# A Fourier mixing layer and a gated feed-forward network in one kernel: the first two chunks of batch 0 take the weights half by half

## The chip, the cores and the metric

The kernel runs on one core of a Trainium2 chip. The core has five engines with queues of their own: TensorE (PE; PEld are its weight loads), VectorE (DVE), ScalarE (ACT), GpSimd (POOL) and SyncE (SP, which here only issues DMAs). They meet through semaphores. The metric is the device time of one execution in microseconds; the median of three runs of the kernel before is 1980.55 (1979.31 to 1981.25).

## The reference

```python
X = np.fft.fft(x, axis=1)            # x: (8, 3008, 256)
X = np.fft.fft(X, axis=2)
a = X.real.reshape(24064, 256)
gate = 1.0 / (1.0 + np.exp(-(a @ w_gate)))       # w_gate, w_val: (256, 1536)
out = gate * (a @ w_val) @ w_out                 # w_out: (1536, 256)
```

The real part of a two-dimensional Fourier transform of each batch goes through a gated network. The weights arrive as 64-bit floats, everything else as 32-bit.

## The kernel before

**Sequence transform.** For each batch the kernel folds x by the symmetries of cosine and sine and multiplies it with a cosine and a sine table `ST` (lines 392 to 440). The results are rows P ("pk"), Q ("qk") and one extra row e for the feature in the middle ("ek", for batch 0 a whole resident tile; for the others a row in memory, `ed`, that is broadcast chunk by chunk into `ek`). For batch 0 this is done at the start, from tables loaded by `load_table` (line 188): the cosine sums first, then the sine sums, and `evacuate` brings each out of PSUM between weight conversions (lines 682 to 693).

**The feature transform is merged into the weights.** `jobs` (line 204) cuts the three weight matrices into 18 pieces of 256 columns or rows: `(0, c)` of w_gate, `(1, c)` of w_val, `(2, c)` of w_out. A piece is loaded by SP (`weight_load`) and converted from 64 to 32 bits in `weight_round`: two ACT operations (lines 261, 262), three DVE operations (271, 272, 274) and one POOL addition (276). A gate or value piece is then merged with the feature table on TensorE (`merge`, line 290: eight matmul records, two ACT copies into `G1` and `G2`, two small DMAs into `ge`). An output piece is used by `forms`: 11 sums (line 317) and 4 copies (line 315, ACT) of 128x128 blocks for each group of three hidden tiles. For groups 0 and 1 the sums run on POOL, for 2 and 3 on DVE, in parts of six and five.

**The main loop.** The sequence is cut into six chunks of 252 rows (the last 246) a batch, and the 1536 hidden columns into 12 tiles of 128. One step `i` is one hidden tile of one chunk, 576 steps in all. Within a step the order is written out by hand:
- `front_a(i)`: two matmuls of P with `G1` into a PSUM bank "pf";
- `part(i)`: for the first 12 steps DVE adds e (line 523, two operations); later ACT copies with scale 2 (line 520), and the bank was filled with e times `ge` by `seed` one step earlier (line 506, ACT);
- `gate_a(i-1)`, `gate_b(i-1)`: sigmoid (539, ACT), difference (541, or 544 from step 12, DVE), product (556, DVE), second sigmoid (557, ACT), product (558, DVE), and after the second and third tile of a group 7 and 6 sums of blocks on POOL (line 562);
- what is due of the weights (`pre`, `use`, `parts_`);
- `back((i-5)//3, (i-5)%3)`: five of the 15 products of a group of three hidden tiles with the forms `wf` of w_out, into the PSUM tiles "po0" to "po4";
- `front_b(i)`: two matmuls of Q with `G2` onto the same bank.

A chunk is four groups, 12 steps. With its last group the five "po" tiles are copied to `C` by ACT (tiles 0, 2, 4) or DVE (1, 3), line 586, and `finish` puts 20 sums (line 609) and four transposes (line 619) of it into `later`; every step takes two or three of these in turn, on DVE. PSUM has eight banks: five are "po", three are shared by "pf" and the merges' "ps". Three resident tiles hold several things in turn: `x4` (x of the next batch, and weight pieces 10 and on), `os` (output, and e of batch 0) and `c` (C, and weight pieces 7 and 8).

**When the weights are due.** Pieces 0 to 8 are converted before step 0. Pieces 9 to 17 are converted at steps 0 to 8, and a gate or value piece among them is merged at steps 4 to 8, two to four steps after its conversion:

```python
for j in range(9, len(jobs)):
    pre.setdefault(j - 9, []).append(lambda j=j: weight_round(j))
    if KEEP <= j < len(jobs) - 3:
        at(j - 9, lambda j=j: weight_load(j + 3))
for j in range(3, len(jobs)):
    w, c = jobs[j]
    i = (0, 1, 4, 7, 9, 10)[c] if w == 2 else 2 * c - 3 + w
```

**Side work.** `at(i, f)` puts work at the end of step i: the copy of the next batch's x in another order through DRAM (`mirror_x`), its load (`load_x(1)` at step 14), seven small loads `e_load`, the same for the tables, the sums of e on TensorE at step 40 (`e_sums`), and folds of x on POOL (`fold_ops`).

Of the kernel before, what the change touches and what calls it, by code (L numbers as in the profile page):

```python
# [7 lines left out]
F32 = mybir.dt.float32  # L8
I32 = mybir.dt.int32
U32 = mybir.dt.uint32  # L10
AF = mybir.ActivationFunctionType
# [66 lines left out]
def kernel(  # L78
# [49 lines left out]
    def mm(o, l, r, start, stop):  # L128
        nc.tensor.matmul(o, l, r, start=start, stop=stop, skip_group_check=True)  # L129
# [57 lines left out]

    def load_table(t, nq):
        for q in range(0, NQ, nq):
            nc.sync.dma_start(out=ST[0][0:NP, t, q : q + nq], in_=stab[:, t, q : q + nq])  # L190

    def mirror_tables():
        return mirrored(tr, stab, NE)
# [1 line left out]
    def table_again():  # L195

        ST[0] = const.tile([P, 2, NQ, NE + NO], F32, name="st", tag="st")
        for t in range(2):
# [2 lines left out]

    jobs = [(w, c - (w == 2)) for c in range(NPR + 1) for w in range(3)
            if (c if w == 2 else c < NPR)]
    RAW, WS = {}, {}
    shared = {}
    KEEP = 10
# [94 lines left out]
    def forms(g):  # L303

        w = [WO[f // 2].rearrange("p f (a h j) -> p f h a j", h=2, j=TB)[:, f % 2]
             for f in range(3 * g, 3 * g + 3)]
        f = wf[:, g].rearrange("p m (a j) -> p m a j", j=TB)
        engine = nc.gpsimd if g < 2 else nc.vector

        def block(i):  # L310
            return w[i // 2][:, i % 2] if i < 6 else f[:, i - 6]

        def some(lo, hi):
            for i, (a, sign) in enumerate(W_COPIES if lo == 0 else ()):
                nc.scalar.mul(f[:, len(W_SUMS) + i], block(a), float(sign))
            for i, (a, b, op) in list(enumerate(W_SUMS))[lo:hi]:
                engine.tensor_tensor(f[:, i], block(a), block(b), op=(ALU.subtract, ALU.add)[op])  # L317
        return [lambda lo=lo: some(lo, lo + 6) for lo in range(0, len(W_SUMS), 6)]


    W = {}
# [157 lines left out]

    chunks = [(k0, min(CH, -(-(NK - k0) // 3) * 3)) for k0 in range(0, NK, CH)]  # L480
    assert NK <= chunks[-1][0] + chunks[-1][1] <= NK + 1 and NFT == 12
    groups = [(b, c, g) for b in range(B) for c in range(len(chunks)) for g in range(NG)]
    H, SF, EK = {}, {}, {}

    def cut(i):
        b, c, _ = groups[i // 3]
        k0, n = chunks[c]
        f = i % NFT
        return PQE[b], slice(k0, k0 + n), n, f, slice(f * P, (f + 1) * P)

    def e_rows(i):

        b, c, _ = groups[i // 3]
        k0, n = chunks[c]
        EK[i // NFT] = ekp.tile([P, CH], F32, name="ek", tag="ek")[:, 0:n]
        nc.sync.dma_start(out=EK[i // NFT], in_=ed[b : b + 1, k0 : k0 + n].to_broadcast([P, n]))

    PF, AP, Z = {}, {}, {}

    def seed(i):  # L500


        _, _, n, f, _ = cut(i)
        PF[i] = bank("pf").rearrange("p (g n) -> p g n", g=2)[:, :, 0:n]
        for g in range(2 if i >= NFT else 0):
            nc.scalar.activation(PF[i][:, g], EK[i // NFT], AF.Copy, scale=ge[:, g, f : f + 1])  # L506

    def front_a(i):
        (pk, *_), ks, _, _, fs = cut(i)
# [59 lines left out]
    def back(p, part):  # L569

        b, c, g = groups[p]
        n = chunks[c][1]
        R = 2 * n // 3
        last = p == len(groups) - 1
        if part == 0 and g == 0:
            PO[:] = [pso.tile([P, 2 * WC], F32, name=f"po{t}", tag=f"po{t}") for t in range(NB)]
        for at_, (hb, wb) in list(enumerate(PRODUCTS))[part * 5 : part * 5 + 5]:
            t, j = divmod(PLACE[at_], 3)
            mm(PO[t][:, j * R : (j + 1) * R], wf[:, g, wb], block(p, hb), g == 0 and at_ % 3 == 0,
               g == NG - 1)  # L580
            if g == NG - 1 and at_ % 3 == 2:
                if t == 0:
                    C[0] = cp.tile([P, 10 * WC], F32, name="c", tag="c")
                    nc.gpsimd.memset(C[0][:, 15 * R : 15 * R + 40], 0.0)
                if not (last and t == NB - 1):
                    (nc.vector.tensor_copy if t == 1 or t == 3 and not last else nc.scalar.copy)(  # L586
                        C[0][:, 3 * t * R : 3 * (t + 1) * R], PO[t][:, 0 : 3 * R])
        if part == 2:
            del H[p], SF[p]
            if g == NG - 1:  # L590
                finish(b, c, last)

    def finish(b, c, last):
# [1 line left out]
        R = 2 * n // 3  # L595
        more = k0 + n > NK
        nb = -(-n // TB)
        t = C.pop(0)
        queues = (nc.sync, nc.scalar) if last else (nc.sync,)
        os_ = []  # L600

# [56 lines left out]
    for j in range(2):  # L658
        weight_load(j)
    load_x(0)  # L660
    load_table(0, NQ // 2)
    for j in range(2, 6):
        weight_load(j)
    load_table(1, NQ)
    for j in range(6, KEEP):
        weight_load(j)

    def weight_round(*js):
        for j in js:
            weight_parts(j)  # L670
            weight_join(j)
# [12 lines left out]
        for sums, _, _ in cos:  # L684
            sums(*range(i * NQ // 2, (i + 1) * NQ // 2))
    sin = [seq_group(0, blk, 1, other.get((blk, 1))) for blk in range(2)]
    for sums, _, _ in sin:
        sums(*range(NQ))
    evacuate = [then for _, then, _ in cos + sin]
    for then, js in zip(evacuate, ((2, 3, 4), (5,), (), (), (6, 7), (8,))):  # L690
        weight_round(*js)
        then()()
    nc.scalar.dma_start(out=ed[0:1], in_=PQE[0][2][0:1])
    nc.vector.tensor_copy(PQE[0][1][0:1, 0:CH], PQE[0][2][0:1, 0:CH])
    for j in range(KEEP, KEEP + 3):
        weight_load(j)
    weight_use(2)
# [5 lines left out]
        side.setdefault(i, []).extend(fs)  # L703

    pre, use = {}, {}
    for j in range(9, len(jobs)):
        pre.setdefault(j - 9, []).append(lambda j=j: weight_round(j))
        if KEEP <= j < len(jobs) - 3:  # L710
            at(j - 9, lambda j=j: weight_load(j + 3))
    for j in range(3, len(jobs)):
        w, c = jobs[j]
        i = (0, 1, 4, 7, 9, 10)[c] if w == 2 else 2 * c - 3 + w
        use.setdefault(i, []).append(lambda j=j: weight_use(j))


# [2 lines left out]
    calm = lambda lo: (i for i in range(lo, count) if 3 <= i % i0 <= 7)  # L720
    for i, f in enumerate(mirror_x(1)):
        at(i0 - 3 + i // 2, f)
    at(i0 + 2, lambda: load_x(1))
    for b in range(1, B):
        at(i0 + 2 + b, lambda b=b: e_load(b))
    for i, f in enumerate(mirror_tables()):
# [1 line left out]
    at(3 * i0, e_fold)  # L728
    at(3 * i0 + 4, lambda: e_sums()())
    at(3 * i0 + 6, table_again)  # L730
    for i in range(i0, count, i0):
        at(i - 8, lambda i=i: e_rows(i))

    for b in range(B - 1):
        s0 = b * per
        g0 = s0 + 3 * i0 + 4 if b else 5 * i0 + 4


        slots = [i for i in range(s0 - 2 * i0 if b > 1 else s0 if b else 2 * i0, g0) if i % i0 < 4]

        def folds(slots, b=b):
            ops = fold_ops(b + 1, 2)
            for i, f in enumerate(ops):
                at(slots[i * len(slots) // len(ops)], f)
        at(slots[0] - 1, lambda slots=slots, folds=folds: folds(slots))
        at(g0 - 2, lambda b=b: seq_start(b + 1))
        for blk in (1, 0):
            at(g0, *[lambda b=b, blk=blk, what=what: whole(b + 1, blk, what)() for what in range(2)])
        if b < B - 2:
            at(g0 + 1, lambda b=b: load_x(b + 2))  # L750
            for i, f in zip(calm(s0 if b else 3 * i0), mirror_x(b + 2)):
                at(i, f)

    for i in range(count):
# [14 lines left out]
        if i >= 5:  # L769
            back((i - 5) // 3, (i - 5) % 3)  # L770
        front_b(i)
        n = 3 if i >= count - 8 else 2 + i % 2
        for f in later[0:n]:
            f()
        del later[0:n]
# [57 lines left out]
```

## Time and profile before

| | |
|---|---|
| median of three runs | 1980.55 us |
| the profiled execution | 1978.69 us |
| its span | 1976.8 us |
| granted TensorE clock, mean | 0.995 |
| TensorE busy | 1932.9 us (98%) |
| DVE busy | 1518.7 us (77%) |
| ACT busy | 1337.7 us (68%) |
| POOL busy | 1631.4 us (83%) |
| TensorE busy, 60 to 90 us | 8.92, 8.16 and 3.46 us of each 10 |
| TensorE busy, 300 to 1900 us | all of it |

The page counts an engine as busy while an instruction runs on it. A line of the timeline has its start, its length, the engine, the line of the code, the operation, what it writes and reads, and in brackets how long the engine sat idle before it and what it waited for. A line of the waits has the waiting engine and line, what released it, the total in us, how often, and the longest. A line of the windows has the stretch, its length, and for each engine the busy time and the number of instructions. One product of 32-bit floats stands as two matmul records, so a front's two matmuls are "x4". Neighbouring lengths overlap by what a pipeline hides, so the time of a thing is best read from start to start.

### The profile page before, as it was taken

What the parts mean: (1) busy time and instruction counts of PE and PEld (TensorE: products, weight loads), DVE (VectorE), ACT (ScalarE), POOL (GpSimd) and SP (SyncE); (2) the same over time, 40 slices, a digit from 0 to 9 for tenths busy, and PEclk for the clock granted to TensorE, in tenths of its full rate; (3) what the DMA queues carried; (4) which work ended last, traced back from release to release, by engine and by line L of the source; (5) the groups of instructions that cost most, each with busy time, mean ns of one, the idle gap of its engine ahead of it and who ended that gap; (6) DMA issues with size and microseconds to landing.
All of it is one profiled execution on the core that took longest, in us unless ns stands there. A gap on an engine that the chain in (4) does not pass through costs nothing.

```text
span 1976.8 us, 34387 instructions
## 1 busy us (share of the span) xinstructions
PE 1932.9 (98%) x11232; PEld 1788.1 (90%) x11232; DVE 1518.7 (77%) x3177; ACT 1337.7 (68%) x3103; POOL 1631.4 (83%) x2858
## 2 busy tenths in 40 slices
PE   6899999999999999999999999999999999999997
PEld 3689889998999899998999989999899999999997
DVE  7788778886787677786778867787678877777777
ACT  3467657775777667775777757777577766777774
POOL 3879888997889878997889868998688996777776
PEclk9999999999999999999999999999999999999999
DMA  7354413112012020212013021211210110011011
GB/s 267 88 132 93 137 31 110 47 26 77 14 47 58 14 78 14 66 39 77 15 25 80 15 78 23 47 49 22 77 20 14 20 21 14 14 19 22 14 19 27
DMA packets 171444, 101.41 MB, mean 51 GB/s; under 512 B 133890, under 2 KB 163204, under 8 KB 168588
## 3 DMA queue, kind: packets, MB, share of 16 engines
q1 hardware_dynamic: 169294, 98.64, 20.5%
q8 instruction: 90, 1.47, 0.3%
q10 hardware_dynamic: 1940, 0.56, 0.1%
q14 instruction: 88, 0.72, 0.1%
q0 software_dynamic: 32, 0.00, 0.0%
HBM read 74.45 MB, written 50.18 MB: 63 GB/s over the span
## 4 chain that ended last, share of the span: by engine, by line
PE 94%; DMA 2%; DVE 2%; ACT 1%; POOL 1%; issue 0%; ACTq 0%; DVEq 0%; SPq 0%; POOLq 0%
PE pf L129 48%; PE po L129 41%; PE ev L129 4%; DMA st<-in_stab_dram 1%; DMA ge<-G 1%; PE ps L129 1%; PE od L129 1%; DVE wf L317 0%; DMA raw<-in_moe_w_val_dram 0%; DVE ae L523 0%; DVE z L541 0%; POOL sf L562 0%; DVE h L558 0%; POOL wf L317 0%; DVE c L609 0%
## 5 line engine op out<-in xcount | busy, mean ns | idle before, releaser
L562 POOL TENSOR_TENSOR sf<-h 128x168 f32<-128x168 f32 (+1 forms) x960 | 549.3, 591 | 222.0 <-DVE h L558 221.9
L562 POOL TENSOR_TENSOR sf<-h,sf 128x168 f32<-128x168 f32 (+1 forms) x1152 | 657.6, 591 | 58.7 <-DVE h L558 58.7
L129 PE MATMUL pf<-qk,G 128*128 128x252 f32 (+1 forms) x2304 | 582.6, 376 | 3.2 <-DVE ae L523 1.9
L129 PE MATMUL pf<-pk,G 128*128 128x252 f32 (+1 forms) x2304 | 582.9, 376 | 0.0
L558 DVE TENSOR_TENSOR h<-z 128x252 f32<-128x252 f32 (+1 forms) x576 | 301.3, 523 | 350.7 <-ACT z L557 350.1
L506 ACT ACTIVATE pf<-ek,ge 128x252 f32<-128x252 f32 (+1 forms) x1128 | 531.5, 471 | 18.5
L129 PE MATMUL po<-sf,wf 128*128 128x168 f32 (+1 forms) x3072 | 530.1, 306 | 0.0
L520 ACT ACTIVATE ae<-pf 128x504 f32<-128x504 f32 (+1 forms) x564 | 332.6, 590 | 234.4 <-PE pf L129 233.6
L609 DVE TENSOR_TENSOR c<-c 128x168 f32<-128x168 f32 (+1 forms) x949 | 484.8, 542 | 5.5 <-ACT c L586 0.3
L129 PEld LDWEIGHTS pf<-pk,G 128*128 128x128 f32 x2304 | 436.3, 190 | 53.0 <-issue 2.3
L129 PEld LDWEIGHTS po<-sf,wf 128*128 128x128 f32 x3072 | 473.0, 190 | 8.5
L129 PE MATMUL po<-h,wf 128*128 128x168 f32 (+1 forms) x2688 | 475.9, 305 | 2.1 <-ACT a L473 1.6
L129 PEld LDWEIGHTS po<-h,wf 128*128 128x128 f32 x2688 | 427.4, 190 | 19.2 <-ACT a L473 2.0
L129 PEld LDWEIGHTS pf<-qk,G 128*128 128x128 f32 x2304 | 409.9, 190 | 30.0 <-DVE ae L523 2.9
L544 DVE TENSOR_TENSOR z<-ae,pf 128x504 f32<-128x504 f32 (+1 forms) x564 | 374.3, 664 | 17.6 <-ACT h L539 17.1
L539 ACT ACTIVATE h<-pf 128x252 f32<-128x252 f32 (+1 forms) x576 | 218.5, 379 | 164.4 <-PE pf L129 152.7
L557 ACT ACTIVATE z<-z 128x252 f32<-128x252 f32 (+1 forms) x576 | 231.1, 401 | 91.0 <-DVE z L544 59.5
L556 DVE TENSOR_TENSOR h<-h,pf 128x252 f32<-128x252 f32 (+1 forms) x576 | 232.2, 403 | 0.0
L562 POOL TENSOR_TENSOR sf<-sf 128x168 f32<-128x168 f32 (+1 forms) x192 | 111.4, 580 | 15.0
L129 PE MATMUL ev<-st,x 63*128 63x376 f32 (+4 forms) x372 | 97.6, 414 | 9.7 <-DVE x L340 8.0
L562 POOL TENSOR_TENSOR sf<-sf,h 128x168 f32<-128x168 f32 (+1 forms) x192 | 106.7, 556 | 0.0
L129 PEld LDWEIGHTS ev<-st,x 63*128 63x128 f32 (+1 forms) x372 | 66.4, 187 | 37.4 <-DVE x L340 8.4
(115 smaller groups left out, 870.0 us busy)
## 6 DMA issues: line engine op xcount, KB each, us to landing
x<-xr SPq DMA_DIRECT2D x14, 1536.0 KB
out_dram<-os SPq DMA_DIRECT2D x380, 56.0 KB
xr<-in_xf_dram SPq DMA_DIRECT2D x14, 768.0 KB
xr<-in_xf_dram SPq DMA_DIRECT2D x35, 256.0 KB
ek<-ed SPq DMA_DIRECT2D x39, 126.0 KB
out_dram<-os SPq DMA_DIRECT2D x288, 7.0 KB
x<-in_xf_dram SPq DMA_DIRECT2D x2, 1512.0 KB
tr<-in_stab_dram SPq DMA_DIRECT2D x2, 1129.5 KB
```

The source lines that it names most:

```text
L129: nc.tensor.matmul(o, l, r, start=start, stop=stop, skip_group_check=True)
L506: nc.scalar.activation(PF[i][:, g], EK[i // NFT], AF.Copy, scale=ge[:, g, f : f + 1])
L520: nc.scalar.activation(AP[i], PF[i], AF.Copy, scale=2.0)
L539: nc.scalar.activation(H[p][:, fh, 0:n], PF[i][:, 0], AF.Sigmoid)
L544: nc.vector.tensor_tensor(z[:, :, ::-1], AP.pop(i), PF[i], op=ALU.subtract)
L556: nc.vector.tensor_tensor(h[:, fh, 0:n], h[:, fh, 0:n], PF.pop(i)[:, 1], op=ALU.mult)
L557: nc.scalar.activation(z[:, 0], z[:, 0], AF.Sigmoid)
L558: nc.vector.tensor_tensor(h[:, fh, n:], z[:, 0], z[:, 1], op=ALU.mult)
L562: nc.gpsimd.tensor_tensor(block(p, dst), block(p, a), block(p, b), op=(ALU.subtract, ALU.add)[op])
L609: engine.tensor_tensor(t[:, dst * R : (dst + 1) * R], *v, op=(ALU.subtract, ALU.add)[op])
```

## The change

The order of the groups in the first two chunks is changed. Chunks 0 and 1 of batch 0 first both take groups 0 and 1 (hidden tiles 0 to 5; steps 0 to 5 and 6 to 11), then both take groups 2 and 3 (steps 12 to 17 and 18 to 23). Each chunk's "po" sums therefore come in two halves: the first half is copied to `C` as before, and the second is added to it by five DVE operations. From step 24 the order is as before. With it:
- `jobs` is in another order: w_out's piece 2 comes eighth (counted from 0), and its pieces 3 to 5 last. Piece 9 is no longer converted at step 0: pieces 9 to 17 are converted at steps 3, 4, 6, 7, 8, 10, 12, 13 and 15, and the gate and value pieces among them are merged three steps later, at 6, 7, 9, 10, 11 and 13.
- `forms` runs on POOL only for group 0, on DVE for 1 to 3, in parts of four, four and three.
- The sine table is loaded in two parts, with pieces 5 and 6 between them; the sine sums run in halves; the conversions between the evacuations are dealt out one by one.
- e for both chunks is taken from the resident tile; its copy in row 0 of Q covers both chunks and is set to zero at step 11, as from step 12 the seed brings e in.
- `load_x(1)` moves from step 14 to 20, the folds of batch 1 start at step 25 (not 24), up to five steps of twelve have one, and below step 48 every step takes three of `later`.

```diff
-    jobs = [(w, c - (w == 2)) for c in range(NPR + 1) for w in range(3)
-            if (c if w == 2 else c < NPR)]
+    jobs = [(0, 0), (1, 0), (0, 1), (1, 1), (2, 0), (0, 2), (1, 2), (2, 1), (2, 2)]
+    jobs += [(w, c) for c in range(3, NPR) for w in range(2)] + [(2, c) for c in range(3, NPR)]
...
-        engine = nc.gpsimd if g < 2 else nc.vector
+        engine = nc.vector if g else nc.gpsimd
...
-        return [lambda lo=lo: some(lo, lo + 6) for lo in range(0, len(W_SUMS), 6)]
+        return [lambda lo=lo: some(lo, lo + 4) for lo in range(0, len(W_SUMS), 4)]
...
-    groups = [(b, c, g) for b in range(B) for c in range(len(chunks)) for g in range(NG)]
+    twice = [(0, 0), (0, 1)]
+    groups = [(*bc, g) for gs in (range(NG // 2), range(NG // 2, NG)) for bc in twice for g in gs]
+    groups += [(b, c, g) for b in range(B) for c in range(len(chunks)) for g in range(NG)
+               if (b, c) not in twice]
...
+        ek = pqe[2][:, ks] if groups[i // 3][:2] in twice else EK[groups[i // 3][:2]]
         PF[i] = bank("pf").rearrange("p (g n) -> p g n", g=2)[:, :, 0:n]
         for g in range(2 if i >= NFT else 0):
-            nc.scalar.activation(PF[i][:, g], EK[i // NFT], AF.Copy, scale=ge[:, g, f : f + 1])
+            nc.scalar.activation(PF[i][:, g], ek, AF.Copy, scale=ge[:, g, f : f + 1])
...
+                dst, src = C[b, c][:, 3 * t * R : 3 * (t + 1) * R], PO[t][:, 0 : 3 * R]
+                if g0 == NG // 2:
+                    nc.vector.tensor_tensor(dst, dst, src, op=ALU.add)
+                elif not (last and t == NB - 1):
...
-    for j in range(2, 6):
+    for j in range(2, 5):
         weight_load(j)
-    load_table(1, NQ)
-    for j in range(6, KEEP):
+    sines = load_table(1, NQ // 2)
+    next(sines)
+    for j in range(5, 7):
+        weight_load(j)
+    next(sines)
+    for j in range(7, KEEP):
         weight_load(j)
...
-    for then, js in zip(evacuate, ((2, 3, 4), (5,), (), (), (6, 7), (8,))):
+    for then, js in zip(evacuate, ((2, 3), (4,), (5,), (6,), (7,), (8,))):
...
+    for j, i in enumerate((3, 4, 6, 7, 8, 10, 12, 13, 15), 9):
+        pre.setdefault(i, []).append(lambda j=j: weight_round(j))
         if KEEP <= j < len(jobs) - 3:
-            at(j - 9, lambda j=j: weight_load(j + 3))
+            at(i, lambda j=j: weight_load(j + 3))
+    for j, i in enumerate((0, 0, 1, 2, 0, 4, 6, 7, 9, 10, 11, 13, 14, 14, 17), 3):
         use.setdefault(i, []).append(lambda j=j: weight_use(j))
...
-    at(i0 + 2, lambda: load_x(1))
+    at(i0 + 8, lambda: load_x(1))
+    at(i0 - 1, lambda: nc.vector.memset(PQE[0][1][0:1, 0 : 2 * CH], 0.0))
...
-        n = 3 if i >= count - 8 else 2 + i % 2
+        n = 3 if i < 4 * i0 or i >= count - 8 else 2 + i % 2
```

## The prediction

> **What bounds the kernel now.** I read the page's busy row by slices first, then the matmul engine's waits, its timeline, and the two queues that it waits for.
>
> The page: TensorE's busy tenths, 49 us a slice.
>
> ```profile
> PE   6899999999999999999999999999999999999997
> ```
>
> Only the first two slices, the second's neighbour and the last have room; elsewhere TensorE is full and nothing else matters. Its waits in the first 300 us:
>
> ```profile
> PE ps L129 <- POOL raw L276: 8.4, 1, 8.4
> PE ev L129 <- DVE x L340: 8.0, 1, 8.0
> PE ps L129 <- POOL wx L276: 7.2, 2, 6.0
> PE pf L129 <- DVE ae L523: 1.9, 2, 1.4
> PE ev L129 <- DMA st<-in_stab_dram: 1.7, 1, 1.7
> PE po L129 <- ACT a L473: 1.6, 1, 1.6
> ```
>
> The first two are the load of x and the first weights, untouched here. The third is a merge waiting for a weight piece that POOL has not joined. TensorE's timeline there:
>
> ```profile
> 81.34 1.12 PE L129 MATMUL pf<-qk,G 128*128 128x252 f32 x4 [0.55 <-DVE ae L523]
> 82.34 1.09 PE L129 MATMUL pf<-pk,G 128*128 128x252 f32 x4
> 89.43 3.78 PE L129 MATMUL ps<-wx,dt 128*128 128x256 f32 x8 [6.00 <-POOL wx L276]
> 93.00 1.74 PE L129 MATMUL po<-sf,wf 128*128 128x168 f32 x10
> ...
> 96.28 1.89 PE L129 MATMUL ps<-wx,dt 128*128 128x256 f32 x8
> 98.01 1.59 PE L129 MATMUL po<-h,wf 128*128 128x168 f32 x10
> 99.43 1.01 PE L129 MATMUL pf<-qk,G 128*128 128x252 f32 x4
> 100.28 1.01 PE L129 MATMUL pf<-pk,G 128*128 128x252 f32 x4
> ```
>
> From the starts: a merge takes 1.73 us, a back part 1.42, each front 0.85. Step 0 begins at 49.78, step 15 at 121.92: 72.1 us. The work in it is 15 pairs of fronts (25.7), 10 back parts (14.2) and 9 merges (15.6), 55.5 us. So 16.7 us are lost, more than the waits show, since the clock also sags (3.78 against 1.89). No choice of order can gain more there. The windows say who is to blame:
>
> ```profile
> core 0: us, PE busy (x) PEld busy (x) DVE busy (x) ACT busy (x) POOL busy (x), PEclk, DMA share, GB/s
> 60.00:70.00 10.00, 8.92 (x39) 6.80 (x38) 9.15 (x19) 5.59 (x15) 9.92 (x18) 1.00 0.21 53
> 70.00:80.00 10.00, 8.16 (x43) 6.86 (x42) 8.30 (x12) 4.54 (x14) 9.84 (x13) 1.00 0.40 104
> 80.00:90.00 10.00, 3.46 (x15) 2.39 (x14) 8.34 (x14) 4.01 (x9) 10.00 (x18) 0.82 0.23 68
> ```
>
> POOL is full, but DVE is nearly so. Relief for POOL that is paid by DVE is no plain gain.
>
> **What the Trainium skill says.** "SBUF — State Buffer", section "Who interferes with whom": a DVE tensor_scalar in a two-port mode, or a DVE operation with two SBUF inputs, contends with GpSimd for a shared port. The trace agrees: the conversion's tensor_scalar takes 0.43 us beside an idle POOL (57.22) and 1.39 beside a busy one (70.48), while L556, with one input in PSUM, stays at 0.40. "TensorE: Matmul & The Clock Gate", section "What's actually happening": an idle window of about 3.4 us halves the clock. The 6.00 us wait agrees; waits of 1 us show no such loss. "DMA: Bandwidth & Descriptors", section "Queues, rings and completion order": completion isn't first in, first out. The sine table, issued at 24.74, lands at 40.39, one microsecond before the piece queued behind it.
>
> **The change, part by part.** All in the profiled execution's time (span 1976.8, time 1978.69, 1.9 below the median 1980.55); I carry differences over.
>
> *Sines in two parts, pieces 5 and 6 behind the first.* TensorE is done with cosines at 38.7 and starts sines at 40.39. The first half now has 1.6 MB less ahead of it or in it (one piece, half a table), 5 us at about 0.3 MB/us: landed before 36. The second half follows a piece later than the table did, about 42; it is wanted 12 matmuls of 0.32 after 38.7, at 42.5. Gain 1.7, or 0 if it is 2 us later; I take 1.6, so step 0 starts at 48.2. Splitting the matmuls adds none.
>
> *Conversions at steps 3,4,6,7,8,10,12,13,15 in place of 0 to 8; merges three steps behind.* A conversion is, on DVE, 1.53 us alone (56.76 to 58.29), 2.3 beside POOL (65.13 to 67.44, 99.00 to 101.33), up to 3.05; on POOL 1.29. The other work of a step below 12 on DVE is 2.5 (58.29 to 60.79): two L523 (0.78), L541 (0.58), L556 and L558 with their wait (1.1). From step 12 it is 1.6. *Forms of group 1 move from POOL to DVE, and all forms come in three parts*: 11 operations cost POOL about 0.5 each (5.5 in all) and DVE 0.42 beside POOL (six in 2.6 from 103.73), so 1.7, 1.7 and 1.3. ACT's four copies (1.0) have idle time to lie in.
>
> Laying this out step by step, TensorE's losses are:
> - Steps 0 to 2: none (3.44 each; DVE 2.5).
> - Step 3: the second front waits for L523: 1.0. Step 4: conversion 9 (2.3) on top of 2.5 against 1.7 of TensorE: 3.4. Step 5: conversion 10 and form part one: 2.5. Steps 7 and 8: 0.6 and 1.0.
>  Together 8.5. Check by totals: steps 0 to 8 ask 36 us of DVE, with about 4 idle at the start, and 30 of TensorE.
> - No merge waits for POOL: piece 11 is joined at 82, merged at 89; 13 at 93 and 97 to 99.
> - But a new wait. Three PSUM banks are shared by the fronts and the merges. Up to step 10 two fronts' banks are live at a merge; at steps 11 and 13 the seed for the next step has already taken the third, so the merge waits for L556 of the step before. At step 11 that stands behind L523 and L541: 2.6 us (at least 1.9, from 0.2 + 0.78 + 0.58 + 0.41); at step 13, 1.0. Behind the merge on TensorE stand the back part and the second front, so it is all lost. 3.6.
> - Steps 14 to 19 give DVE conversion 17, 22 form operations and 1.6 a step: the back part of step 17 waits 1.2 for the ninth form operation of group 2, step 20's 0.65 for group 3's. 1.9.
>
> Sum 14.0 against 16.7: with the sines, 4.3 us ahead at step 21.
>
> *Twelve half-weight groups for two chunks.* The matmuls are the same in number. First halves leave PSUM as whole chunks did (three ACT copies, two DVE). Second halves add five DVE operations of 128x504 each, bound by the L544 row (0.664): 10 × 0.6 = 6 us, in steps 20 to 28. C is allocated twice at once; the pool has two buffers and the pieces in one are gone by step 6. The row of e taken from the resident tile instead of a broadcast costs ACT the same; one broadcast less on SP. The copy of row 0, 504 instead of 252 wide (0.74), and the memset at step 11 lie in DVE idle time before a second front; if not, 0.5.
>
> *Later sums three a step below step 48.* Both chunks' 48 sums and transposes fall in steps 22 to 37 where before 2.5 a step went with gaps. DVE: 16 × 1.6 + 40 × 0.50 + 8 × 0.38 + 9 × 0.6 = 54, against 16 × 3.13 = 50. DVE may lag: step 14 of the kernel before finished its gate 1.4 us late and cost 0.5. Some 2.7 of slack leaves 1.3; folds on POOL from step 25 make the sums 0.62 (169.61: three in 2.57), for 3.5. I take 2.2, range 0 to 6.
>
> At step 40 the sums of e stand on the path:
>
> ```profile
> 204.48 0.67 DVE L586 COPY c<-po 128x504 f32<-128x504 f32 x1
> 205.07 1.40 DVE L609 TENSOR_TENSOR c<-c 128x168 f32<-128x168 f32 x2
> ...
> 208.06 1.69 PE L129 MATMUL po<-h,wf 128*128 128x168 f32 x10 [1.61 <-ACT a L473]
> ...
> 210.84 1.12 PE L129 MATMUL pf<-qk,G 128*128 128x252 f32 x4 [1.08 <-ACT ae L520]
> ```
>
> A third L609 goes ahead of them: 0.5, and three a step behind: 0.5. I take 1.0.
>
> *DMA order.* load_x(1) moves from step 14 to 20, past six e_loads on SP (2 us of the queue each) and the weight pieces; ge's issues move with the merges. x needed some 13 us (issued 126.95, DMA quiet near 140); now issued near 135, wanted by POOL at 151. Hidden, with 3 us to spare. C's memset moves on POOL: 0.13.
>
> Forecast: 4.3 − 2.2 − 1.0 = 1.1 us less: **1979.4**, own range 1976.6 to 1984.5, within what a measurement can tell from nothing (0.2%, 4 us).
>
> **Rivals.** *Faster by 6 to 11, about 1973.* POOL carries less, so DVE meets it less. Were conversions 9 to 13 at 1.53, steps 3 to 8 would lose 5 × 0.8 less (4.0), the bank waits 1.5 less, and the lag be swallowed (2.2): 8 us gained. For it: the tail runs three sums a step at 2.9 us without a wait. Against: POOL works 7.7 us per 9.4 in sums of h.
> *Slower by 4 to 7, about 1986.* DVE overflows in steps 21 to 37: with sums at 0.62, 54 + 5 = 59 against 53 for the 17 steps, with no slack left from step 20, and 1 us of clock sag at step 4: 7.5 + 1 + 1 − 4.3 = 5. It decides from about 0.57 a sum on.
> *x comes late.* If the six e_loads hold SP or the rings 3 us longer, POOL stands at step 25, and each microsecond beyond its 3 of slack is lost: −4 to +8, about 1984. Against it: XR is complete by then.
> *It doesn't do what it says*, the merge still waiting for POOL: three steps and 7 us of distance speak against it; kept in the forecast.
>
> **How the numbers follow.** Forecast 0.43, faster rival 0.35, DVE overflow 0.15, late x 0.07. Faster by 0.2%: 0.35; same 0.43; slower 0.22. The bounds of the unknown costs, DVE beside POOL above all, put the range at 1970 to 1987.
>
> **What would show it.** Right: no wait of ps for POOL at L276; ps waiting for DVE L556 (or L541) twice, about 2.6 and 1; pf waiting for L523 three to five times, 8 us in all; DVE busy above 95% in steps 22 to 37. Step 15 near 116, step 21 near 136.4 against 140.7. Wrong: step 15 before 112 (contention oversized), or after 119.

## The result, and the profile after

The kernel after the change takes 1983.69 us (median of 20 executions, 1981.31 to 1989.97), the kernel before beside it 1980.62 (20 executions, 1978.87 to 1982.73): a ratio of 1.0017, with a 95% interval of 1.0010 to 1.0024. The change costs about 3.1 us. The forecast was 1979.4, a gain of 1.1. The time lies inside the range and inside the forecast's own range, and just inside what was called no difference (0.2%), but on the other side of zero, and the interval leaves out zero.

The profiled execution of the kernel after took 1985.5 us (span 1983.6). That is 1.8 above its median, while the profiled execution before was 1.9 below its own. The two profiles therefore differ by 6.8 us, and some 3.7 of that is the luck of two executions. What follows has to be read with this in mind: a profile shows places, the medians show sizes.

The page of the kernel after, TensorE's busy tenths: the third slice, 99 to 149 us, has lost one tenth, and nothing else has moved.

```profile
PE   6889999999999999999999999999999999999997
```

TensorE's waits in its first 300 us. Columns: the waiting engine and line, what released it, the total, how often, the longest. (L531 was L523 before, L277 was L276, L565 was L557, L318 was L317, L474 was L473.)

```profile
PE ps L129 <- POOL raw L277: 8.4, 1, 8.4
PE pf L129 <- DVE ae L531: 7.5, 3, 3.8
PE ev L129 <- DVE x L341: 7.0, 1, 7.0
PE ps L129 <- ACT z L565: 4.4, 2, 2.4
PE pf L129 <- ACT ae L528: 4.0, 3, 1.6
PE po L129 <- DVE wf L318: 2.5, 2, 1.8
PE po L129 <- ACT a L474: 1.6, 1, 1.6
```

The change does what it says: the merge's wait for POOL's join (7.2 us) is gone, and so is the wait for the sine table (1.7). Four kinds have come in their place: the second front waits for DVE's L531 (1.9 has become 7.5), the merges wait for a bank (4.4), the second front waits for ACT's copy L528 (4.0, which includes the one at step 41 that was there before, 1.08 then and 1.64 now), and a back part waits for forms (2.5). TensorE's timeline places them:

```profile
66.68 1.12 PE L129 MATMUL pf<-qk,G 128*128 128x252 f32 x4 [2.81 <-DVE ae L531]
73.84 2.05 PE L129 MATMUL pf<-qk,G 128*128 128x252 f32 x4 [3.77 <-DVE ae L531]
75.68 1.89 PE L129 MATMUL pf<-pk,G 128*128 128x252 f32 x4
...
102.96 3.57 PE L129 MATMUL ps<-wx,dt 128*128 128x256 f32 x8 [1.96 <-ACT z L565]
115.29 1.97 PE L129 MATMUL ps<-wx,dt 128*128 128x256 f32 x8 [2.42 <-ACT z L565]
132.37 1.12 PE L129 MATMUL po<-h,wf 128*128 128x168 f32 x6 [1.84 <-DVE wf L318]
172.96 1.12 PE L129 MATMUL pf<-qk,G 128*128 128x252 f32 x4 [0.99 <-ACT ae L528]
177.75 1.12 PE L129 MATMUL pf<-qk,G 128*128 128x252 f32 x4 [1.37 <-ACT ae L528]
218.15 1.12 PE L129 MATMUL pf<-qk,G 128*128 128x252 f32 x4 [1.64 <-ACT ae L528]
```

In order these are the second fronts of steps 4 and 5, the first front of step 6, the merges of steps 11 and 13, the back part of step 17, and the second fronts of steps 29, 30 and 41, the last behind the sums of e. Three things are to be seen. The matmul after the 3.77 runs 2.05 instead of 1.12, and the next front 1.89 instead of 1.01: the clock is slow there, and so it is in the merge of step 11 (3.57 against 1.97). The two merges are put down to ACT's L565, but that instruction reads nothing of PSUM; DVE's product L564, the reader of the bank, ran at 102.41 and 114.74 for 0.4 us and ended just before the merges began. And the waits of steps 29 and 30 stand alone; the other steps from 21 to 39 have none.

DVE's timeline at steps 4 and 5, the largest wait of all:

```profile
68.34 1.25 DVE L272 TENSOR_SCALAR wx<-wx 128x512 f32<-128x512 f32 x1 [0.20 <-ACT wx L262]
69.62 0.43 DVE L273 TENSOR_SCALAR wx<-wx 128x512 int32<-128x512 int32 x1
70.08 0.69 DVE L275 SCALAR_TENSOR_TENSOR wx<-wx 128x512 int32<-128x512 int32 x1
70.69 0.49 DVE L318 TENSOR_TENSOR wf<-wc 128x128 f32<-128x128 f32 x2
71.21 1.79 DVE L318 TENSOR_TENSOR wf<-wf,wc 128x128 f32<-128x128 f32 x2
72.93 0.85 DVE L531 SCALAR_TENSOR_TENSOR ae<-ek,ge,pf 128x252 f32<-128x252 f32 x2
```

A conversion (2.35 us) and the first part of the forms (2.24) stand ahead of L531, with no gap between them; the second front begins when L531 ends. Ten microseconds earlier the same engine had room. The windows of the kernel after (stretch, length, then busy time and instructions of each engine, granted clock, DMA share, GB/s):

```profile
50.00:60.00 10.00, 10.00 (x49) 8.86 (x48) 5.97 (x13) 4.50 (x16) 5.05 (x12) 1.00 0.44 152
60.00:70.00 10.00, 6.24 (x31) 4.90 (x29) 8.41 (x15) 4.79 (x13) 9.22 (x15) 1.00 0.01 0
70.00:80.00 10.00, 6.23 (x17) 5.06 (x17) 9.15 (x21) 1.70 (x5) 5.08 (x8) 0.66 0.19 53
```

From 50 to 60 DVE is busy 5.97 of 10 us while TensorE is full; from 60 to 80 DVE is nearly full and TensorE idle more than a third of the time.

The stretches of the two profiles side by side, measured from the start of one step to the start of another:

| stretch | before, us | after, us | difference | forecast |
|---|---|---|---|---|
| start to step 0 | 49.8 | 49.7 | −0.1 | −1.6 |
| steps 0 to 15 | 72.1 | 72.8 | +0.7 | −4.6 |
| steps 15 to 21 | 18.8 | 21.9 | +3.2 | +1.9 |
| steps 21 to 41 | 64.6 | 67.7 | +3.0 | +2.2 |
| steps 41 to 44 | 12.7 | 13.3 | +0.6 | +1.0 |
| the rest | 1758.7 | 1758.2 | −0.5 | 0 |
| span | 1976.8 | 1983.6 | +6.8 | −1.1 |

With the prices of a front, a back part and a merge from the kernel before, the work of steps 0 to 15 is again 55.5 us. The loss there is 17.3, where 12.1 was forecast. The bare waits in it are 11.9 us (0.96, 2.81, 3.77, 1.96 and 2.42). In the kernel before they were 11.5 of a loss of 16.7: the 7.2 and 1.9 of the prediction's list, and three that the list left out,

```profile
PE ps L129 <- ACT G L298: 1.3, 3, 0.6
PE ps L129 <- POOL sf L562: 0.6, 1, 0.6
PE po L129 <- DVE wf L317: 0.5, 1, 0.5
```

Of the 5.2 us that remain there, 1.9 are slow clock (the merge of 3.78 us and the back part behind it). The rest is put down here to what nine stops of TensorE cost beyond their waits.

### The profile page after: what moved, and what is told of

Read it like the earlier page. It is cut to its first block, busy times and chain, and to the rows that moved or that the text cites. A ratio compares the mean times of both kernels' runs of the same rounds, so it can differ in the third digit from the quotient of the medians.

```text
span 1983.6 us, 34372 instructions
## 1 busy us (share of the span) xinstructions
PE 1937.3 (98%) x11232; PEld 1791.8 (90%) x11232; DVE 1527.7 (77%) x3199; ACT 1336.0 (67%) x3103; POOL 1625.5 (82%) x2847
## 4 chain that ended last, share of the span: by engine, by line
PE 95%; DVE 3%; DMA 1%; ACT 1%; issue 0%; SPq 0%; DVEq 0%; ACTq 0%
PE pf L129 48%; PE po L129 40%; PE ev L129 5%; PE ps L129 1%; PE od L129 1%; DMA x<-in_xf_dram 1%; DVE c L622 1%; DVE wf L318 0%; ACT z L565 0%; DVE z L552 0%; DVE h L566 0%; DVE ae L531 0%; DVE c L597 0%; ACT pf L514 0%; DVE wx L275 0%
## 5 line engine op out<-in xcount | busy, mean ns | idle before, releaser
L129 PE MATMUL pf<-qk,G 128*128 128x252 f32 (+1 forms) x2304 | 583.7, 376 | 11.5 <-DVE ae L531 7.5
L528 ACT ACTIVATE ae<-pf 128x504 f32<-128x504 f32 (+1 forms) x564 | 332.5, 590 | 229.9 <-PE pf L129 229.6
L565 ACT ACTIVATE z<-z 128x252 f32<-128x252 f32 (+1 forms) x576 | 231.3, 402 | 105.7 <-DVE z L552 77.3
L564 DVE TENSOR_TENSOR h<-h,pf 128x252 f32<-128x252 f32 (+1 forms) x576 | 231.8, 402 | 0.0
```

The costliest lines, as they stand in the source:

```text
L528: nc.scalar.activation(AP[i], PF[i], AF.Copy, scale=2.0)
L564: nc.vector.tensor_tensor(h[:, fh, 0:n], h[:, fh, 0:n], PF.pop(i)[:, 1], op=ALU.mult)
L565: nc.scalar.activation(z[:, 0], z[:, 0], AF.Sigmoid)
```

## The experiments

Each is an edit of the kernel after unless it says otherwise. The kernel before was run beside each of four sets of experiments (medians 1980.64 for e1 to e4, 1980.41 for e5 to e8, 1980.32 for e9 to e11 and 1981.05 for e12), so the column to compare is the difference to before. A ratio's interval reaches 0.0006 to 0.0013 to either side, 1.2 to 2.6 us. The ratio is not the quotient of the two medians and differs from their difference by up to 1.2 us (e3: 1.6 by the medians, 2.8 by the ratio). Differences under some 2 us between two experiments are therefore not settled by this table. Of e8 there are six executions, of e9 and e10 five each.

| kernel | median, us | ratio to before, 95% | to before, us | step 0 to 21 in its profile, us |
|---|---|---|---|---|
| the change | 1983.69 | 1.0017 (1.0010 to 1.0024) | +3.1 | 94.8 |
| e1: seeds after the merges | 1982.06 | 1.0007 (0.9999 to 1.0015) | +1.4 | 92.8 |
| e2: two conversions early | 1980.36 | 1.0000 (0.9992 to 1.0008) | −0.3 | 90.8 |
| e3: forms of group 1 on POOL | 1982.22 | 1.0014 (1.0007 to 1.0021) | +1.6 | 91.1 |
| e4: sines whole | 1984.11 | 1.0019 (1.0011 to 1.0026) | +3.5 | 91.6 |
| e5: products that keep TensorE busy | 1983.99 | 1.0022 (1.0015 to 1.0028) | +3.6 | 93.4 |
| e6: conversions from step 0, merges by 10 | 1976.16 | 0.9984 (0.9975 to 0.9992) | −4.3 | 85.1 |
| e7: later sums dealt out | 1983.58 | 1.0021 (1.0012 to 1.0030) | +3.2 | 94.8 |
| e8: e6 and e7 | 1975.20 | 0.9972 (0.9961 to 0.9983) | −5.2 | 85.7 |
| e9: e8, forms of group 1 on POOL | 1973.15 | 0.9963 (0.9951 to 0.9976) | −7.2 | 83.5 |
| e10: e8, forms of group 1 from step 5 | 1971.76 | 0.9961 (0.9949 to 0.9974) | −8.6 | 83.3 |
| e11: e8, sines whole | 1977.80 | 0.9987 (0.9980 to 0.9993) | −2.5 | 86.2 |
| e12: the kernel before with halved sines | 1978.72 | 0.9988 (0.9982 to 0.9995) | −2.3 | |

The theory after the comparison was this: the idea of the change is sound, but its conversions start three steps too late (DVE idles in steps 0 to 2 and is then the bound), two of its merges come where the seed has already taken the third bank, and the forms that DVE was given fall on the same steps as the late conversions. The rivals: that the slow clock after the waits, rather than the waits, makes the loss; that the halved sines gain nothing; and that DVE overflows with the later sums in steps 21 to 37.

### e1: the seed after the merge at steps 11 and 13

```diff
+        late = i in (i0 - 1, i0 + 1)
-        if i0 <= i + 1 < count:
+        if i0 <= i + 1 < count and not late:
             seed(i + 1)
...
+        if late:
+            seed(i + 1)
         if i >= 5:
```

> The changed kernel, with the seed of the next step written after the merge at steps 11 and 13, so that the merge takes the free third bank and the seed the one that L564 frees. Bank theory: the two waits of ps at steps 11 and 13 (2.0 and 2.4 us) and the slow clock of the merge behind the first (1.6 us) are gone from the trace; some of it comes back as a wait for DVE in steps 14 to 20, so 3 to 6 us off 1983.7, about 1979. Rival, DVE is the bound of steps 9 to 20 anyway: the waits move to the fronts or the back parts of the same steps and the time stays within 1 us of 1983.7.

The merges wait no more. The fronts behind them do, for the seed, which now comes late. TensorE's timeline of e1:

```profile
113.42 1.12 PE L129 MATMUL pf<-pk,G 128*128 128x252 f32 x4 [1.39 <-ACT pf L514]
122.35 1.77 PE L129 MATMUL pf<-pk,G 128*128 128x252 f32 x4 [2.41 <-ACT pf L514]
```

These are the first fronts of steps 14 and 16. 1.96 and 2.42 have become 1.39 and 2.41, the slow clock has moved along (the back part behind the second takes 2.66 in place of 1.59), and the form wait of step 17 falls from 1.84 to 0.60. The median is 1.7 us nearer to before, which the two intervals don't tell from nothing; 3 to 6 us had been expected. The trace shows that the waits of `ps` were for a bank and not for data: nothing but the order in which the bank was asked for has changed. Turning the order round won back only 0.6 of their 4.4 us.

### e2: pieces 9 and 10 converted at steps 0 and 2

```diff
-    for j, i in enumerate((3, 4, 6, 7, 8, 10, 12, 13, 15), 9):
+    for j, i in enumerate((0, 2, 6, 7, 8, 10, 12, 13, 15), 9):
```

> The changed kernel, with pieces 9 and 10 converted at steps 0 and 2 instead of 3 and 4, in DVE's idle time. DVE theory: the wait of 3.8 us at step 5 falls to about 1 and that of 2.8 at step 4 to about 1, and with gaps that short the clock doesn't sag at steps 5 and 6 (2.8 us): 5 to 7 us off, about 1977.5. Rival, the clock sags for a reason of its own (it also fell behind a wait of 2.0 us at step 11): then only 3 to 4 us, about 1980. Second rival, what is won early is lost again at steps 9 to 20, where DVE and the bank waits bound: within 1.5 us of 1983.7.

Two numbers, and 3.4 us less: the loss of the change is gone, within 1.6 us. In steps 0 to 2 DVE is busy 8.5 of 10.8 us in place of 6.3 of 10.3. The wait at step 5, in e2's timeline:

```profile
75.54 1.12 PE L129 MATMUL pf<-qk,G 128*128 128x252 f32 x4 [1.26 <-DVE ae L531]
```

3.77 has become 1.26, and after it the clock is full. Step 3 now waits 2.32 in place of 0.96, since the conversion of step 2 lies ahead of it; the three waits fall from 7.5 to 4.5. The two bank waits stay (2.29 and 2.42), as they should. The gain is that of the first rival (3 to 4 us) and not the 5 to 7 expected, but not for its reason: at steps 5 and 6 the clock held. Part of what is missing is the wait that came at step 3.

### e3: the forms of group 1 back on POOL

```diff
-        engine = nc.vector if g else nc.gpsimd
+        engine = nc.gpsimd if g < 2 else nc.vector
```

> The changed kernel with the forms of group 1 back on POOL. If their move to DVE is what cost steps 4 to 6, the wait at step 5 falls by the 2.2 us of the first part and the clock may hold: 2 to 5 us off 1983.7. If POOL's relief was needed, sums of h come late and a wait of po for POOL or ps for POOL appears: 0 to 5 us more. I lean to the first, about 1981.

The wait at step 5 falls from 3.77 to 1.53, and a back part at 85.61 waits 1.59 for POOL's forms instead. The median gains 1.5, the ratio 0.6, and neither is clear of the noise; 2 to 5 had been expected. That the forms cost time on DVE where they meet the conversions is seen in the trace and not shown in the time.

### e4: the sine table whole again

```diff
-    for j in range(2, 5):
+    for j in range(2, 6):
         weight_load(j)
-    sines = load_table(1, NQ // 2)
-    next(sines)
-    for j in range(5, 7):
-        weight_load(j)
-    next(sines)
-    for j in range(7, KEEP):
+    for _ in load_table(1, NQ):
+        pass
+    for j in range(6, KEEP):
         weight_load(j)
...
-    for i in range(2):
-        for sums, _, _ in sin:
-            sums(*range(i * NQ // 2, (i + 1) * NQ // 2))
+    for sums, _, _ in sin:
+        sums(*range(NQ))
...
-    for then, js in zip(evacuate, ((2, 3), (4,), (5,), (6,), (7,), (8,))):
+    for then, js in zip(evacuate, ((2, 3, 4), (5,), (), (), (6, 7), (8,))):
```

> The changed kernel with the sine table loaded whole and the conversions dealt as before the change. If halving the sines gains what the wait before was (1.7 us), step 0 starts 1 to 1.7 us later than in the changed kernel relative to the end of the cosines, and the time is 1 to 1.7 us above 1983.7. If it gains nothing, within 0.7 us of it. Start of step 0 in the trace: 49.65 in the changed kernel, 49.78 before; the end of the cosines tells whether chance in their clock hid the gain.

The edit also turns back the dealing of the conversions between the evacuations. The wait for the table is back in its profile (2.66 at 41.91, and the six sums behind it take 3.63 us in place of 2.14, at a slow clock; step 0 at 53.0 in place of 49.7), but the median is only 0.4 above that of the change. With two intervals of 0.0007 to either side, a gain of anything from nothing to 2 us by the halves is left open by this run; e11 and e12 below narrow it.

### e5: ten products more, to keep the clock

Ten products of 128x168 into a tile of "po" that the back part of step 7 starts afresh, before the second front of step 5. They leave the output as it is.

```diff
             back((i - 5) // 3, (i - 5) % 3)
+        if i == 5:
+            for _ in range(10):
+                mm(PO[4][:, 0:168], wf[:, 0, 12], block(0, 0), True, True)
         front_b(i)
```

> The changed kernel with ten more products of 128x168 (2.85 us of TensorE) in the gap of 3.8 us at step 5, into a bank that the next group starts afresh; nothing else moves, and the output is the same. Clock theory: the gap shrinks to about 1 us of idle time, fronts and merge of steps 5 and 6 run at full speed whenever the gap of step 4 has not already slowed them, and the time falls by 1.5 to 2.8 us, to about 1981.5, with a narrower spread of single runs. Rival, the slow matmuls have nothing to do with idle time: no change, or 0 to 1 us more.

No gain: 3.6 us slower than before, where the change was 3.1. In its profile the clock had fallen already at 66 us, behind the wait of 2.81 at step 4 (0.55 and 0.59 from 66 to 70), so the products came too late for that and in part ran at the slow clock themselves. From step 5's second front on the clock was full, and steps 0 to 21 took 93.4 us in place of 94.8, but nothing of it is seen in the median. As a test of the slow clock this run is weak.

The means of the granted clock say more: 0.9942 over the executions of the change, 0.9936 over the 146 of the kernel before. Within one kernel, executions with a lower clock are longer (a correlation of −0.66 after, −0.43 to −0.69 before). But at the same mean of 0.993, 0.994 or 0.995 the median of the change is still 2.7 to 4.2 us longer. This speaks against the slow clock as the whole cause of the shift. It doesn't decide, because the mean also counts stretches in which TensorE is idle, as from 18 to 22 us in the profile after (0.50).

### e6: conversions from step 0, no merge after step 10

```diff
-    for j, i in enumerate((3, 4, 6, 7, 8, 10, 12, 13, 15), 9):
+    for j, i in enumerate((0, 1, 3, 4, 6, 7, 9, 11, 12), 9):
...
-    for j, i in enumerate((0, 0, 1, 2, 0, 4, 6, 7, 9, 10, 11, 13, 14, 14, 17), 3):
+    for j, i in enumerate((0, 0, 1, 2, 0, 4, 3, 4, 6, 7, 9, 10, 13, 13, 16), 3):
```

> The changed kernel with the conversions of pieces 9 to 17 at steps 0, 1, 3, 4, 6, 7, 9, 11 and 12 and the six merges at 3, 4, 6, 7, 9 and 10, before any seed takes the third bank; pieces of w_out used one step earlier. Bank and DVE theories together: no wait of ps for L564 or for the bank; the waits of the back parts for form operations at steps 17 and 20 shrink to under 1; the fronts' waits in steps 3 to 8 stay at 4 to 7 us since DVE still has the work. Step 0 to step 21 then takes about 85 us (94.8 in the changed kernel, 90.9 before), the time is about 1976. Rival, DVE bounds steps 0 to 20 whatever the order: 90 us and about 1980.

This takes away the cause of the bank waits rather than the order: the merges end before the seeds take the third bank, and each is still three steps behind its conversion. 4.3 us faster than before, 7.3 better than the change (3.2 and 6.5 by the ratios), as expected. No merge waits more than 0.33 us for a bank, and no `po` for forms. Three smaller waits are new: 1.05 at step 12 for the memset that now falls behind a conversion, and 0.90 and 0.41 at steps 15 and 17. What is left of the DVE waits of steps 3 to 5 is a single one, in e6's timeline:

```profile
75.12 1.12 PE L129 MATMUL pf<-qk,G 128*128 128x252 f32 x4 [4.24 <-DVE ae L531]
```

A conversion of 2.9 us beside POOL (69.14 to 72.06) and the forms' first part (71.98 to 74.30) lie ahead of it on DVE.

### e7: the later sums dealt out where the adds fall together

```diff
-        n = 3 if i < 4 * i0 or i >= count - 8 else 2 + i % 2
+        n = {27: 2, 28: 1}.get(i, 3) if i < 3 * i0 + 3 or i >= count - 8 else 2 + i % 2
```

> The changed kernel with two later sums at step 27 and one at 28 instead of three, where the second halves' additions fall too, and from step 39 on two and three in turn as before the change. Theory of the overflowing DVE queue: the two waits of fronts at steps 29 and 30 (1.0 and 1.4 us) and the 0.3 us about each fall to under 1 us together, the sums of e at step 40 lose 0.5 us: 2 to 3 us off 1983.7, about 1981.2. Rival, the additions themselves overfill it: under 1 us.

At steps 27 to 30 the adds of the second half (L597, 0.6 each) and three of `later` meet on DVE. The copy L528, for which TensorE waits, stands on ACT behind a sigmoid that waits for DVE; in the timeline of the kernel after, at step 29:

```profile
171.75 0.41 ACT L565 ACTIVATE z<-z 128x252 f32<-128x252 f32 x1 [2.37 <-DVE z L552]
```

With three of `later` moved on, the two waits (0.99 and 1.37) become one of 0.68, and steps 21 to 41 take 66.1 us in place of 67.7. The wait after the sums of e grows by 0.25. In the median nothing of it is seen (+3.2 against +3.1, where 2 to 3 us less had been expected), which an effect of about 1.3 us within intervals of 1.6 allows. The trace shows the mechanism; its size in the median stays open.

### e8, e9, e10: the parts together, and the forms at another step

e8 is e6 and e7. e9 adds the edit of e3 to it; e10 instead uses w_out's piece 2, and so starts the forms of group 1, one step later:

```diff
-    for j, i in enumerate((0, 0, 1, 2, 0, 4, 3, 4, 6, 7, 9, 10, 13, 13, 16), 3):
+    for j, i in enumerate((0, 0, 1, 2, 0, 5, 3, 4, 6, 7, 9, 10, 13, 13, 16), 3):
```

> The two edits before this one together. If they add, 2 to 3 us below the one with early merges alone, about 1973.5, faster than both kernels. If the lag of DVE in steps 14 to 21 is what the later sums build on, they don't add, about 1976.

> The version with early merges and dealt sums, with the forms of group 1 back on POOL. If DVE still bounds steps 4 to 8 there, the gap of 4.4 us at step 5 shrinks by about 2 and the time falls by 1 to 3 us from 1975.2; if POOL becomes the bound, back parts or merges wait for it and the time rises by 0 to 3. With the gap at step 5 the largest left, I expect 1974.

> The same version with w_out's piece 2 used at step 5 instead of 4, so that the three parts of group 1's forms fall in steps 5 to 7 and step 4 has only its conversion. DVE theory: the gap at step 5 falls from 4.4 to about 2.7, and 0 to 1 us comes back at steps 7 and 8; the time is 0.7 to 1.7 us under 1975.2, about 1974.

e8 is 5.2 us faster than before, e9 7.2, e10 8.6. e8 gains 1.0 on e6 by the medians and 2.4 by the ratios, where 2 to 3 had been expected if the parts add; e9 gains some 2 on e8, as expected, and e10 3.4 (2.2 by the ratios), where 0.7 to 1.7 had been. None of these steps from one to the next is clear of the intervals. The wait at step 5 is 4.37 in e8, 2.14 in e9 and 2.00 in e10; e10's timeline has it as

```profile
71.88 1.12 PE L129 MATMUL pf<-qk,G 128*128 128x252 f32 x4 [2.00 <-DVE ae L531]
```

and 0.88 at 86.82 in addition. e10 leaves the forms on DVE and is no slower than e9, which takes them away (1.4 us faster by the medians, 0.4 by the ratios): for the wait at step 5 it does as much to start the forms a step later as to move them to another engine. e10 beats both kernels, with 0.9961 (0.9949 to 0.9974).

### e11, e12: what the halved sines are worth

e11 is e8 with the edit of e4. e12 is the kernel before with that part of the change alone: the table in two loads with pieces 5 and 6 between them, and the sums in halves, while the conversions stay dealt as before.

```diff
-    for j in range(2, 6):
+    for j in range(2, 5):
         weight_load(j)
-    load_table(1, NQ)
-    for j in range(6, KEEP):
+    sines = load_table(1, NQ // 2)
+    next(sines)
+    for j in range(5, 7):
+        weight_load(j)
+    next(sines)
+    for j in range(7, KEEP):
         weight_load(j)
...
-    for sums, _, _ in sin:
-        sums(*range(NQ))
+    for i in range(2):
+        for sums, _, _ in sin:
+            sums(*range(i * NQ // 2, (i + 1) * NQ // 2))
```

> The same version with the sine table loaded whole and the conversions before step 0 dealt as before the change. If halving the sines gains its 1.7 us where nothing later hides it: about 1976.7. If what it gains at the first half it loses at the second (which waited 1.2 to 2.7 us in two of the profiles so far): within 0.8 us of 1975.2. I expect the second.

> The kernel before with one part of the change alone: the sine table in two loads with pieces 5 and 6 between them, and the sine sums in halves. The prediction's term says 1.6 us less (1979.0 against 1980.6), the wait for the table (1.7) gone and step 0 starting near 48.2 instead of 49.8. If the gain is what the changed kernel showed when the parts were put together again (0.4), it is 1980.2, which can't be told from no change; if it is what the reordered kernel showed (2.6), it is 1978.0. A second half of the table that lands late would show as a wait of up to 2.7 us in the sine sums and no gain.

e11 loses 2.7 us against e8 (+0.8 at most had been expected: a miss), and e12 gains 2.3 on the kernel before (1.0 to 3.6). The forecast's 1.6 is inside both readings, and e4's 0.4 is inside its margin of e12's. So the halves do gain about 2 us, which e12 shows by itself; e4 and e11 also change the dealing of the conversions. The profile of a single execution need not show it: in e12's, the second half of the table landed late,

```profile
44.18 0.90 PE L129 MATMUL ev<-st,x 126*128 126x377 f32 x2 [1.48 <-DMA st<-in_stab_dram]
```

and step 0 began at 50.30, no earlier than before. Over the profiles of halved kernels this wait was nothing in most, and 0.7, 1.2, 1.5 and 2.7 us in four; step 0 began between 48.1 and 53.9 in these eleven, at 49.7 in the mean, and at 49.8, 53.0 and 53.0 in the three with the whole table. An order of loads has to be judged by medians.

## Why the prediction was wrong by its sign and right in its parts

*Reading of the bound: right.* Only the first 230 us moved. After step 44 the two profiles take 1758.7 and 1758.2 us.

*The merge no longer waits for POOL: right.* No `ps` is released by L277 after the first weights, and the rival "it doesn't do what it says" falls. *x does not come late: right.* TensorE shows no wait for it.

*Sines, 1.6 gained: right in size, in part by luck.* The profile after shows no gain at step 0, but e12 measures 2.3 and e11 2.7, e4 only 0.4. The forecast took one short wait for the whole table (1.7) as its price; the two other profiles with the whole table have 2.7 and 2.6 and a slow clock behind them, and the second half comes late more often than the forecast allowed. (The prediction says that completion isn't first in, first out; its own example, the table landing one microsecond before the piece behind it, is in order.)

*DVE late at steps 3 to 8: mechanism right, size wrong.* Forecast 1.0, 3.4, 2.5, and 1.6 at steps 7 and 8, together 8.5. Measured waits: 0.96, 2.81, 3.77, none at steps 7 and 8, together 7.5; but steps 0 to 8 take 37.5 us for 26.6 of work, 10.9 lost. About 0.3 us more than its wait is lost at each stop, and some 2.8 is the slow clock in steps 5 and 6, which the forecast put at nothing (only its slower rival had 1 us for it). The term for the forms' part was 1.7 and measured 2.24; the conversion was 2.3 and measured 2.35. So the contention of DVE with POOL, on which the faster rival rested, was sized rightly, and that rival falls for the change as made: of conversions 9 to 13 only one came down to about 1.5 (from 85.87), the others took 2.2 to 2.4.

*Bank waits at steps 11 and 13: mechanism right, size wrong.* Forecast 2.6 and 1.0, measured 1.96 and 2.42 as waits, 4.4 for 3.6. With 1.6 of slow clock in the merge of step 11 and the stops, steps 8 to 15 lose 6.5 us. At step 13 the forecast doesn't name the conversion, 112.17 to 114.15, that stands on DVE ahead of the gate's difference at 114.15, behind which L564 had to wait. At step 11 it named the wait and made it 0.6 too long.

*Forms at steps 17 and 20: right, a little small.* Forecast 1.2 and 0.65, measured 1.84 and 0.61; the stretch loses 3.2 in place of 1.9.

*Later sums, 2.2: near (2.9), but by another mechanism.* The forecast, and the rival of DVE's overflow, spread it over 16 steps; DVE is indeed busy 94% of steps 22 to 37 (above 95% was forecast), but TensorE waited only at steps 29 and 30, where the adds of the second half and three sums meet. The rival's 7.5 us didn't come; its own figures, 59 against 53, give 6. *The sums of e:* forecast 1.0, measured 0.55.

*The step that failed* is the comparison "14.0 against 16.7". The 14.0 is a sum of bare waits, and the 16.7 is everything that TensorE lost: 11.5 us of waits and 5.2 of slow clock and of stops that cost more than their wait. The prediction had noted that 16.7 was "more than the waits show", and then put the same two things at nothing in its own sum. In the profile after, the waits of steps 0 to 21 are 14.4 us, so the 14.0 was right as a sum of waits, though in part by luck: steps 7 and 8 lost nothing where 1.6 was forecast, step 4 lost less, and steps 5, 13 and 17 lost more. The loss was 20.5, because 6.1 us came on top, 4.4 of it slow clock. Waits set against waits would have given 2.5 us more in place of 2.7 less, and with the other terms as they stood (an estimate from these figures) 4.1 us more in all, where 3.1 was measured. Step 15 was forecast near 116, and 119 was named as the point from which the prediction is wrong; it began at 122.5.

How much of the 6.1 us the median has is not known: the profile after is the sixth longest of 20 executions, and the slow clock differs from one to the next (in e3 and e4 the merge of step 11 runs at full speed).

*What the change could have brought.* The prediction counted the idle time of DVE at the start (4 us) and did not draw the consequence: conversions that start at step 3 leave it idle for three steps and make it the bound for the next three. e2 (3.4 us better), e6 (7.3) and e10 (11.7) show that. The faster rival's number, about 1973, is what the same groups give in e10 (1971.8), with two tuples and the dealing of the later sums changed, but not by the rival's mechanism: a conversion of e6 still takes 2.9 us beside POOL.

*Not settled.* How the 3.1 us of the median divides among the waits and the slow clock behind them, since of the single effects (1.7, 3.4 and 1.5) only the second is clear of its interval; and how much of the dealing of the later sums (e7) reaches the median.

## What to carry to other kernels

When work is moved from one engine to another, write down for every step what the receiving engine has to do before the next instruction that the bound engine waits for; a total over eight steps that fits hides a queue of two long items at one step. When the loss of a kernel is measured from start to start, compare it only with a forecast that has in it all that such a loss has: the waits, what a stop costs beyond its wait, and the slow clock. Where the bound engine shares a few banks, the time at which a bank is asked for counts, not only the time at which its data is ready: end the merges before the next user begins to reserve. And where work must be spread, begin it in the first idle step and not in the first step that needs it.

## What the runs showed of the hardware

Waits well short of 3 us sometimes slow the clock and sometimes don't. At step 11 a wait of 1.96 (the change), 1.97 (e7), 2.27 (e5) or 2.29 (e2) was followed by a merge of 3.57, 3.53, 3.51 and 3.20 us; a wait of 2.34 (e3) or 2.27 (e4) at the same place by one of 1.97. At step 13 a wait of 2.42 never slowed it, in six kernels. At step 4 a wait of 2.80 was followed by a front of 2.05 us in e4, and one of 2.81 by a front of 1.12 in the change, e1, e3 and e7. The Trainium skill, "TensorE: Matmul & The Clock Gate", section "What's actually happening", has a window of about 3.4 us that runs free, with a halved clock after an idle one. The granted clock of 0.50 from 74 to 78 us agrees. A window that doesn't start with the wait could account for the mixture, which no run here tests. If the window had to be idle throughout, a wait of 1.96 would not be enough; it was, and the measurement decides. The prediction's "waits of 1 us show no such loss" holds, but the forecast did not reckon with waits of 2 to 4 us that do.

A stop of TensorE cost some 0.3 us more than the wait that is shown: the two waits at steps 29 and 30 add up to 2.36, and these steps took 2.9 us longer than their 3.13 each, at full clock.
